# Linear attention and a PReLU feed-forward on one core: the order of the first loads, the layout of four solved values, and two engines changed in the opening stage

## The chip, the cores and the metric

The kernel runs on one core of a Trainium2 chip. The metric is the device time of one execution in microseconds; before the change the median of three runs is 665.36 us. The engines are named as in the profile: PE (TensorE; PEld is its weight load), DVE (VectorE), ACT (ScalarE), POOL (GpSimd) and SP (SyncE, which here only issues DMAs). A trailing q, as in SPq, is an engine's instruction queue.

## The reference

The first half is delta-rule linear attention over 4 batches, 8 heads, 768 tokens and head dimension 48; the second half is a feed-forward block with a learned negative slope on the 3072 tokens of width 384.

```python
k_n = k / (norm(k, axis=-1) + 1e-06)
for t in range(768):
    y[:, :, t] = einsum('bhd,bhde->bhe', q_t, state)
    v_old = einsum('bhde,bhd->bhe', state, k_t)
    state = state + beta_t * einsum('bhd,bhe->bhde', k_t, v_t - v_old)
x = y as (3072 tokens, 384)
h = x @ w_in                                   # 384 x 2048
g = maximum(h, 0) + alpha * minimum(h, 0)
out = g @ w_out                                # 2048 x 384
```

All is 32-bit floating point.

## The kernel before, in words

**Tiling.** The recurrence is cut into 12 chunks of 64 tokens (C = 64). A step n is one chunk of two batches, so there are 24 steps; steps 2c and 2c+1 are chunk c. Within a chunk the recurrence is a triangular system: it needs the products of the chunk's keys with each other, the inverse of a lower triangular matrix, and products with the state. When both steps of a chunk are through, `to_ffn` turns its 256 tokens, and the feed-forward of that chunk runs: `ffn_in` (PE L1070, then ACT L1080 and DVE L1082 for the slope) and `ffn_out`. Nearly all the time is this feed-forward on PE, into which the attention of later chunks is woven.

**Order.** All five engine queues are in the order in which the Python code calls the instructions (`manual_schedule`); an engine whose next instruction waits holds up all behind it. Semaphores are set by the framework from the tiles that an instruction reads and writes, buffers that share a tag among them.

**The opening stage** is the first 50 us or so. What matters of it, in program order:

- *First loads.* Keys (`load_early`), beta, queries (`load_q`), values (`load_v`) and 512 KB pieces of w_in (`fetch_in`) go out on SP, one queue. The slopes alpha (`al_sb`, L1668) go out after the sixth piece of w_in. `al_sb` shares the tag "prod" with the scratch tile that `eliminate_small` uses on DVE. `load_late` then fetches the keys a second time, in the layout that the state update needs (tile kl).
- *Keys.* For steps 0 to 3: square, transpose, products of the keys (L472), of which DVE and ACT pick the 16x16 blocks on the diagonal (`pick`) and ACT copies the rest (`raw`) into the tiles `beyond`, which live in `sums`; POOL multiplies them by beta (`weigh_below`, L640).
- *Slopes and queries.* `slopes` transposes alpha on PE (L335); then come the transposes of the queries (`flips`, L416), the products of queries and keys (`queries`, L1549), ACT's copy of them (L1555) and POOL's masking (L1559). `scale_first` (POOL, L840) multiplies the values of a step by beta.
- *`busy(BUSY)`* (L1534): BUSY products of 128x512 of tile kl with the identity, whose result nobody reads. A half in BUSY is a product of half the width. `short(n)` issues n such products of 32x32.
- *`begin_in(6)`*: the weights arrive as 64-bit words, whose two halves ACT converts (L227 the low one, L229 the high one); `convert` then has DVE shift (L243) and POOL add (L250) to finish a piece in two steps.
- *`eliminate_small`* inverts the 16x16 blocks on DVE: a transpose (L652), 14 pairs of a product (L669) and an addition (L675), ones on the diagonal (L681, on POOL), and a transpose back. `place_small(n, by_vector)` spreads the inverse of step n to its place by one DVE instruction (L698) or by four on ACT (L704).
- *`first_chunk`* solves steps 0 and 1: `matrix` (PE product, ACT copy L878), `own_values` (PE product, DVE copy L889), three rounds of `one_round` (PE product by L852, DVE addition L907), then `outputs` (L925). A product here is 16 matmuls, 32 rows in the profile. Half of the heads sit in the other half of the partitions, so a round needs its operands turned: `turn_matrix` makes the turned half of the matrix (two copies of 64x256), `turn_values` a second set of the values (one copy of 128x192 and two of 64x192), on ACT (L865) or POOL (L867) as the call says. `step_spaces` says where these tiles lie.
- *`second_pair`* does the same for steps 2 and 3, woven into the feed-forward of chunk 0. From step 4 on a different path (`attention`, `burst_a`, `burst_b`) is used; before each step there `scale_v` multiplies the step's 128x384 values by the norms (DVE, L778), 20 times in all.

The functions that the change touches, with the profile's line numbers:

## Time and profile before

| | before |
|---|---|
| median of three runs (lowest, highest) | 665.36 us (665.34, 666.39) |
| the profiled execution: time, span | 662.88 us, 661.1 us |
| PE busy in the span | 632.1 us (96%) |
| DVE, ACT, POOL busy | 483.4, 261.3, 136.7 us |
| first product of the keys' inverse (`matrix` of step 0) starts | 33.96 us |
| `matrix` of step 1 starts | 37.78 us |
| `outputs` of step 0 starts | 47.09 us |
| HBM traffic | 31.56 MB read, 4.72 MB written |

The span runs from the first to the last instruction of the program; the execution's own time is 1.78 us more. Times within the profile count from the start of the span. The profiled execution is 2.48 us below the median of the runs. A row of the timeline reads: start, duration, engine, line, operation, output<-inputs, partitions x elements, number merged into the row, and in brackets the idle time of the engine before it and what ended it.

### The profile page before, as it was taken

Reading aid. Unit: us, or ns where it says so; the run is one execution under the profiler, and the core shown is the slowest. Engines: PE = TensorE matmul, PEld = TensorE weight load, DVE = VectorE, ACT = ScalarE, POOL = GpSimd, SP = SyncE. Lnnn points to the kernel's source line nnn. Section 1 sums busy time; section 2 is a strip of 40 time slices with the busy share of each in tenths; the row PEclk is TensorE's granted clock in tenths of the full one; section 3 lists DMA queues with packets and bytes.
Section 4 is the critical chain, followed back from the end, with each engine's and each line's share of the span. In section 5 each row is a group of like instructions: output and inputs, shape, how many; then the busy total and the mean of one; then the engine's idle time right before and its main releaser. Section 6 shows DMA issues by size and latency. Waiting matters only on the chain.

```text
span 661.1 us, 21374 instructions
## 1 busy us (share of the span) xinstructions
PE 632.1 (96%) x9147; PEld 560.7 (85%) x9147; DVE 483.4 (73%) x1140; ACT 261.3 (40%) x610; POOL 136.7 (21%) x258
## 2 busy tenths in 40 slices
PE   5569998999999999999999999999999999999997
PEld 4367777656688988998998998988999999999997
DVE  5535779987899869758959748858968658568383
ACT  6366745434554252243343242232245245042140
POOL 5444744410000000001000000000035044053260
PEclk9979999999999999999999999999999999999999
DMA  9862854311332122122112112112111210100000
GB/s 212 206 177 51 225 126 120 83 28 32 66 77 51 26 54 45 26 50 49 28 38 37 27 37 38 26 38 38 26 42 33 43 34 2 29 10 1 25 1 25
DMA packets 111151, 37.67 MB, mean 57 GB/s; under 512 B 104224, under 2 KB 107440, under 8 KB 111056
## 3 DMA queue, kind: packets, MB, share of 16 engines
q1 hardware_dynamic: 109184, 35.81, 24.3%
q8 instruction: 72, 1.18, 0.7%
q10 hardware_dynamic: 1872, 0.49, 0.4%
q14 instruction: 23, 0.19, 0.1%
HBM read 31.56 MB, written 4.72 MB: 55 GB/s over the span
## 4 chain that ended last, share of the span: by engine, by line
PE 86%; DVE 5%; ACT 4%; SPq 2%; DMA 1%; issue 1%; POOL 0%; ACTq 0%; DVEq 0%; POOLq 0%
PE p_ffn L1070 22%; PE p_ffn L1135 17%; PE p_more L1387 8%; PE p_ffn L1113 5%; PE p_more L1303 5%; PE p_ffn L1293 3%; PE p_ffn L1387 3%; PE p_pair L416 3%; PE p_pair L801 2%; PE p_ffn L1298 2%; PE p_pair L741 2%; PE p_pair L925 2%; PE p_pair L912 2%; PE p_pair L852 2%; PE p_pair L472 2%; PE p_pair L789 1%
## 5 line engine op out<-in xcount | busy, mean ns | idle before, releaser
L1070 PE MATMUL p_ffn<-xt,w_in 128*128 128x256 f32 x768 | 176.5, 383 | 3.3 <-DVE sums L1082 1.6
L1070 PEld LDWEIGHTS p_ffn<-xt,w_in 128*128 128x128 f32 x768 | 142.2, 190 | 24.4 <-issue 2.3
L1082 DVE SCALAR_TENSOR_TENSOR act<-act,al_t,p_ffn 128x256 f32<-128x256 f32 x112 | 48.5, 474 | 26.2 <-ACT act L1080 26.0
L1080 ACT ACTIVATE act<-p_ffn 128x512 f32<-128x512 f32 x56 | 33.3, 595 | 83.2 <-PE p_ffn L1070 83.0
L1327 POOL TENSOR_TENSOR k_t<-k_t 128x128 f32<-128x128 f32 (+1 forms) x48 | 29.0, 604 | 166.4 <-ACT k_t L1322 163.9
L557 DVE TENSOR_TENSOR block<-block,prod 128x30 f32<-128x30 f32 (+9 forms) x150 | 54.2, 362 | 5.2
L551 DVE TENSOR_TENSOR prod<-block 128x30 f32<-128x30 f32 (+9 forms) x150 | 51.9, 346 | 1.6
L405 POOL TENSOR_TENSOR beta_t<-beta_t,rec 128x8 f32<-128x8 f32 x20 | 5.2, 260 | 225.0 <-DVE rec L399 215.4
L1135 PE MATMUL p_ffn<-w_out,act 128*128 128x192 f32 x288 | 49.6, 328 | 0.0
L1135 PEld LDWEIGHTS p_ffn<-w_out,act 128*128 128x128 f32 x288 | 46.6, 190 | 0.3
L968 ACT COPY xt<-p_pair 128x384 f32<-128x384 f32 x22 | 10.4, 479 | 90.8 <-PE p_pair L964 76.9
L1327 POOL TENSOR_TENSOR block<-block 128x128 f32<-128x128 f32 (+1 forms) x48 | 27.9, 582 | 17.3 <-ACT block L1322 14.8
L1293 PE MATMUL p_ffn<-xt,w_in 128*128 128x256 f32 x96 | 28.7, 380 | 0.0
L753 ACT COPY inv<-p_pair 32x256 f32<-32x256 f32 x40 | 14.5, 361 | 24.9 <-DVE u L916 24.1
L793 ACT COPY y<-p_pair 128x384 f32<-128x384 f32 x22 | 10.4, 479 | 33.0 <-PE p_pair L789 31.4
L1341 DVE SCALAR_TENSOR_TENSOR act<-block,al_t,act 128x256 f32<-128x256 f32 x32 | 19.1, 637 | 5.4 <-ACT block L1337 5.4
L1155 DVE TENSOR_TENSOR o_sb<-u,p_ffn 128x192 f32<-128x192 f32 x24 | 7.9, 350 | 20.5 <-PE p_ffn L1135 20.0
L820 DVE TENSOR_TENSOR r<-v_raw,p_pair 64x192 f32<-64x192 f32 (+1 forms) x60 | 21.2, 353 | 2.2 <-PE p_pair L801 1.2
L1341 DVE SCALAR_TENSOR_TENSOR act<-k_t,al_t,act 128x256 f32<-128x256 f32 x32 | 22.3, 735 | 0.1
L949 DVE TENSOR_TENSOR beside<-beside,p_pair 48x384 f32<-48x384 f32 (+1 forms) x36 | 19.8, 549 | 2.9 <-PE p_pair L941 2.7
L1387 PE MATMUL p_more<-w_out,act 128*128 128x192 f32 x128 | 21.9, 329 | 0.0
L1113 PE MATMUL p_ffn<-w_out,act 128*128 128x384 f32 x64 | 21.6, 490 | 0.0
(285 smaller groups left out, 1404.6 us busy)
## 6 DMA issues: line engine op xcount, KB each, us to landing
qp<-in_q_dram SPq DMA_DIRECT2D x48, 96.0 KB, 3.0
v_raw<-in_v_dram SPq DMA_DIRECT2D x48, 96.0 KB, 3.0
kl<-in_k_dram SPq DMA_DIRECT2D x96, 48.0 KB, 2.7
out_dram<-o_sb SPq DMA_DIRECT2D x90, 48.0 KB, 1.6
space_out<-in_moe_w_out_dram SPq DMA_DIRECT2D x11, 384.0 KB, 4.1
ke<-in_k_dram SPq DMA_DIRECT2D x43, 96.0 KB, 3.1
w_out<-in_moe_w_in_dram SPq DMA_DIRECT2D x6, 512.0 KB, 6.3
w_out<-in_moe_w_out_dram SPq DMA_DIRECT2D x5, 384.0 KB, 4.5
```

The costliest lines, as they stand in the source:

```text
L551: nc.vector.tensor_tensor(out=prod, in0=r[:, 0:j, j : j + 1].to_broadcast([128, j, n]), in1=r[:, j : j + 1, j + 1 : HB].to_broadcast([128, ...
L557: nc.vector.tensor_tensor(out=r[:, 0:j, j + 1 : HB], in0=r[:, 0:j, j + 1 : HB], in1=prod, op=ALU.add)
L1070: nc.tensor.matmul(p_h[:, i], w_in[:, t, (f + i) * 128 : (f + i + 1) * 128], xt[:, t], start=(t == 0), stop=(t == KT - 1),)
L1080: nc.scalar.activation(g, p_h, ACT.Relu, scale=-1.0)
L1082: nc.vector.scalar_tensor_tensor(out=g[:, i], in0=g[:, i], scalar=al_t[:, f + i : f + i + 1], in1=p_h[:, i], op0=ALU.mult, op1=ALU.add,)
L1113: nc.tensor.matmul(p_o[u], gs[f // 2][:, f % 2, u * 128 : (u + 1) * 128], w_out[:, f], start=(f == 0), stop=(f == FT - 1),)
L1135: nc.tensor.matmul(p, x(i), w(i), start=(i == 0), stop=(i == FP - 1))
L1293: nc.tensor.matmul(p[:, f * 256 : f * 256 + 256], w(2, f), xt[:, 2], start=True, stop=False)
L1303: nc.tensor.matmul(q[:, j], a, b, start=True, stop=True)
L1327: nc.gpsimd.tensor_tensor(out=dst, in0=a, in1=b, op=ALU.add)
L1341: nc.vector.scalar_tensor_tensor(out=g[:, f], in0=r[:, f], scalar=al_t[:, 2 * i + f : 2 * i + f + 1], in1=g[:, f], op0=ALU.mult, op1=ALU.add,)
L1387: nc.tensor.matmul(p, x(i), w(i), start=(i == 0), stop=(i == FP - 1))
```

## The change

- **Loads.** alpha goes out right after the first keys, into a piece of the tile `rest` of its own (shown as "turned" in the profile) and no longer into a buffer of the tag "prod". The values go out before all pieces of w_in; the pieces follow, six at once. Piece seven is asked for a little earlier.
- **Order on the engines.** ACT's negation of the mask `minus` and POOL's `weigh_below` for all steps stand earlier in the order; seven short products stand ahead of `busy`, and BUSY is 6.5 in place of 6.0. Five pieces of w_in are begun on ACT ahead of the solve, not six, and one at its end, not two; three are still finished in it, the steps of which stand at other places.
- **Elimination.** The ones on the diagonal are written by DVE after the last pair, not by POOL after the first.
- **Placing.** `place_small` of step 1 is by DVE; those of steps 2 and 3 stand in `first_chunk`, on ACT as before, not in `second_pair`.
- **Values in three parts.** The solved values z of steps 0 to 3 lie in one tile of three parts: even heads, odd heads, odd heads turned. A round reads parts 0 and 1 or, by a stride of two, parts 0 and 2, so that the copy of 128x192 in `turn_values` falls away and only two copies of 64x192 are left. They are no longer written back over the raw values, and turned matrices are made by other engines (step 0 on ACT, step 1 on POOL).
- **`scale_v`** runs on POOL.

```diff
 W_IN_P = 512
-BUSY = 6.0
+BUSY = 6.5
 EARLY = 8
...
     load_early(2, (nc.scalar, nc.sync))
-    al_sb = work.tile([FT, 128], FP32, name="al_sb", tag="prod", bufs=2)
...
             )
-            if j == 1:
-
-                ones = flat.rearrange("p (s e) -> p s e", s=2)[:, :, :: LB + 1]
-                nc.gpsimd.memset(ones, 1.0)
+        nc.vector.memset(flat.rearrange("p (s e) -> p s e", s=2)[:, :, :: LB + 1], 1.0)
         own = work.tile([128, NJ * H, HB], FP32, name="inverse", bufs=1)
...
             nv[n] = v_raw.pop(n)
-            nc.vector.tensor_tensor(
+            nc.gpsimd.tensor_tensor(
                 out=nv[n], in0=nv[n],
...
         m, turned_m, z, u = step_spaces[n]
-        z, u = (
-            x[:, 0 : H * D].rearrange("p (a g d) -> p a g d", a=2, g=G) for x in (z, u)
+        return (
+            m.rearrange("p (a g i) -> p a g i", a=2, g=G),
+            turned_m.rearrange("p (g i) -> p g i", g=G),
+            z.rearrange("p (a g d) -> p a g d", a=3, g=G),
+            u.rearrange("p (a g d) -> p a g d", a=2, g=G),
         )
-        m = m.rearrange("p (a g i) -> p a g i", a=2, g=G)
-        return m, turned_m[:, 0 : G * C].rearrange("p (g i) -> p g i", g=G), z, u
...
         crossing(p, [x[:, 0], x[:, 1]], rhs_[n], True)
-        return [lambda: nc.vector.tensor_copy(out=by_parity(nv[n]), in_=p)]
+        return [lambda: nc.vector.tensor_copy(out=step_space(n)[2][:, 0:2], in_=p)]
...
     def turn_values(n, engine):
-        z, turned_z = by_parity(nv[n]), step_space(n)[2]
-        copy_by(engine, turned_z[:, 0], z[:, 0])
-        swapped(engine, turned_z[:, 1], z[:, 1])
+        z = step_space(n)[2]
+        swapped(engine, z[:, 2], z[:, 1])
...
         p = region(p, G * D, g=G)
-        m, turned_m, turned_z, u = step_space(n)
-        z = by_parity(nv[n])
+        m, turned_m, z, u = step_space(n)
+        z, turned_z = z[:, 0:2], z[:, 0:3:2]
         if i == 2:
...
-    def unit(x):
-        return x.rearrange("p h c -> p (h c)")
-
-    step_spaces = {
-        n: [first_words[:, 2048 * n + at : 2048 * n + at + 512] for at in (0, 512, 1024, 1536)]
-        for n in range(2)
-    }
-    step_spaces[2] = [unit(x) for x in (inv[0], mid[0], inv[1], mid[1])]
-    step_spaces[3] = [unit(x) for x in beyond]
+    def step_words(x, at=(0, 512, 768, 1344)):
+        return [x[:, i : i + n] for i, n in zip(at, (512, 256, 576, 384))]
+
+    step_spaces = {n: step_words(first_words[:, 2048 * n :]) for n in range(2)}
+    step_spaces[2] = [
+        *step_words(first_words, (2560, 3648, 3072))[:3],
+        mid[0].rearrange("p h c -> p (h c)")[:, 0 : H * D],
+    ]
+    step_spaces[3] = step_words(sums.rearrange("p i s e -> p (i s e)"))
     for x in beyond:
...
         place_small(0, True)
-        place_small(1, False)
+        place_small(1, True)
...
-        def round_(n, i):
-            return one_round(n, i, ps_big()[:, :, 0:WY])
-
         now(matrix(0, ps_big()[:, :, 0 : G * C]))
-        convert(2)
+        convert(1)
+        turn_matrix(0, nc.scalar)
         z_0 = own(0)
-        m_1 = matrix(1, ps_big()[:, :, 0 : G * C])
         now(z_0)
         turn_values(0, nc.gpsimd)
-        now(m_1)
+        now(matrix(1, ps_big()[:, :, 0 : G * C]))
+        turn_matrix(1, nc.gpsimd)
         z_1 = own(1)
-        convert(1)
         now(z_1)
-        turn_matrix(0, nc.scalar)
         turn_values(1, nc.scalar)
-        convert(1)
-        turn_matrix(1, nc.scalar)
+        convert(2)
         for i in range(3):
-            rounds = [round_(n, i) for n in both]
+            rounds = [one_round(n, i, ps_big()[:, :, 0:WY]) for n in both]
             for x in rounds:
...
             if i == 0:
-                convert(2)
+                place_small(2, False)
+        convert(3)
         load_v(3)
-        begin_in()
+        place_small(3, False)
         y_0 = outputs(0, ps_big()[:, :, 0:WY])
...
     load_early(NKE)
+    al_sb = rest[:FT, 0:128]
+    nc.sync.dma_start(out=al_sb, in_=moe_alpha.rearrange("(f p) -> f p", p=128))
     for n in range(2):
         load_q(n)
-    fetch_in(4)
     for n in range(2):
...
     fetch_in(6)
-    nc.sync.dma_start(out=al_sb, in_=moe_alpha.rearrange("(f p) -> f p", p=128))
...
     norms(3)
+    first_roots(1)
     now(copy_3)
-    first_roots(1)
     gram_2 = gram(2)
...
     raw(1, gram_1)
+    fetch_in(7)
+    weigh_below(1)
     now(later_signs)
...
     load_v(2)
+    nc.scalar.mul(minus, minus, -1.0)
     for i in range(2):
...
     mask = queries()
-    weigh_below(1)
-    nc.scalar.mul(minus, minus, -1.0)
     for i in range(2):
...
         load_q(i + 2)
-
-    busy(BUSY)
-    begin_in(6)
-    eliminate_small()
     for n in range(2, NJ):
         weigh_below(n)
+
+    short(7, ps_one())
+    busy(BUSY)
+    begin_in(5)
+    eliminate_small()
...
             scale_first(i)
-            place_small(i, False)
         alongside(2, 1)
...
```

## The prediction

> **What bounds the kernel now.** I read the page first, for where PE is idle, then the chain of waits, the timeline of the opening stage, and counts of instructions by stretch.
>
> ```profile
> span 661.1 us, 21374 instructions
> ...
> PE 632.1 (96%) x9147; PEld 560.7 (85%) x9147; DVE 483.4 (73%) x1140; ACT 261.3 (40%) x610; POOL 136.7 (21%) x258
> ...
> q8 instruction: 72, 1.18, 0.7%
> ```
>
> PE is busy for 632.1 of 661.1 us. Of the 29 us left, PE's own list of waits has only 1.3 us after 104.5 us (0.6, 0.5 and 0.2), and from 44.61 to 104.5 us about 5 us. So the feed-forward runs at PE's pace, and what can be won lies before 45 us. My yardstick is the start of `outputs` of step 0 (PE L925), 47.09 us: what moves it moves the end, unless a later engine falls behind. The chain up to there:
>
> ```profile
> 14.78 3.70 SPq L210
> 18.48 0.04 issue
> 18.52 0.43 SPq L210
> 18.95 0.04 issue
> 19.00 4.47 DMA al_sb<-in_moe_alpha_dram
> ...
> 36.56 1.17 ACT inv L704 x4
> ...
> 42.76 1.85 issue
> ```
>
> Alpha, 8 KB, is issued at 19.00 us because SP has queued six weight pieces and the values ahead of it. PE, in order, stands on its transpose from 14.44 us, and the queries behind it wait too. Later the chain goes through ACT, which has twelve conversions of 0.6 to 0.7 us queued ahead of the four copies of L704. At 42.76 us PE stops for 1.85 us with nothing to wait for.
>
> ```profile
> 23.61 0.26 PE L335 MATMUL p_pair<-ident,al_sb 16*128 16x16 f32 x1 [9.16 <-DMA al_sb<-in_moe_alpha_dram]
> 23.90 0.27 DVE L669 TENSOR_TENSOR prod<-block 128x112 f32<-128x112 f32 x1 [2.54 <-PE p_pair L335]
> 27.98 5.39 PE L1534 MATMUL p_pair<-kl,ident 128*128 128x512 f32 x12 [0.33 <-DMA kl<-in_k_dram]
> 31.72 1.18 DVE L652 STREAM_TRANSPOSE inverse<-block 128x256 f32<-128x256 f32 x2 [3.34 <-POOL block L681]
> 37.78 1.13 PE L852 MATMUL p_pair<-inv,sums 64*64 64x64 f32 x32 [2.67 <-ACT inv L704]
> ```
>
> The reader should see four stalls that the change addresses: 9.16 us of PE; 2.54 us of DVE, because `al_sb` shares its scratch buffer; 3.34 us of DVE, because the ones on the diagonal queue on POOL behind the masking; and 2.67 us of PE. They are not in series, so their sum is not the gain.
>
> **The change, part by part.**
>
> *Alpha and queries.* Alpha is issued at 5.32 us; with its 4.47 us it lands before 10. The transpose then waits for its PSUM bank, which ACT's last copy of L645 frees at 16.32. So L335 moves from 23.61 to 16.4, and with it the query work (1.95 + 1.97 us) to an end at 20.4 and ACT's two copies L1555 to 21.6. ACT's ten conversions (0.67 + 0.68 us a piece, less overlap 6.4 us) end at 28, ahead of need. The negated `minus` (0.27 us) and `weigh_below` move within idle time of ACT (7.57 us before L336) and of POOL (6.13 us before L1559).
>
> *DVE's elimination.* It starts at 17.45 as before. Undisturbed, its 28 instructions take about 7.9 us by the rows (eight in 1.97, the last sixteen in 4.49, four between at about 0.32), so it would end at 25.3, not 28.39. But POOL's work moves under it: L840 (3.51 us) from 16.1, since the values land by 14; L1559 (2.50 us) from 21.1; two of L640 (1.7 us). The trace shows what this costs:
>
> ```profile
> 100.86 1.03 POOL L250 TENSOR_TENSOR w_out<-w_out 128x384 uint32<-128x384 uint32 x1 [1.26 <-ACT w_out L227]
> 100.92 1.08 DVE L557 TENSOR_TENSOR block<-block,prod 128x84 f32<-128x84 f32 x1
> ```
>
> A DVE instruction of 0.23 us takes 1.08, until POOL's ends. Under L840 at 19.45 to 21.36, DVE got four instructions done in 1.9 us, one for each of POOL's. With one per POOL instruction, 13 are done at 25.4 and the other 15 (4.2 us) at 29.6. Then ones on DVE (0.15 at most, POOL's price), the transposes 1.18, and L698 twice at 0.87: the inverse of step 0 at 31.8, of step 1 at 32.7, against 33.81 and 37.72 now. Without any blocking it would be 27.5; with POOL's 7.7 us all added, 35.2 for step 0. I take 31.8, worked out from the overlap that is shown.
>
> *The filler.* PE must finish `busy` before `matrix` of step 0. It reads tile kl, whose bytes follow the same transfers as before, so it lands only as much earlier as DMA wasted time: the DMA share from 18 to 20 us is low after the 3.70 us issue stall, and two pieces landed late. I put kl at 26.4, about midway between 25.5 (both losses made good) and 27.84 (as now). The filler's 13 half products cost 5.39/12 = 0.45 us each, 5.84 us, at full clock. But PE will have been idle from 20.9 to 26.4. After such idling the granted clock halves for 3.4 us:
>
> ```profile
> 38.00:41.00 3.00, 3.00 (x112) 2.89 (x112) 0.83 (x2) 2.12 (x6) 0.41 (x1) 0.50 0.92 313
> 42.00:44.50 2.50, 0.54 (x15) 0.40 (x13) 0.98 (x3) 1.06 (x2) 1.29 (x1) 1.00 0.76 293
> 45.00:48.00 3.00, 3.00 (x111) 3.00 (x107) 1.66 (x3) 0.00 (x0) 1.43 (x3) 0.50 0.25 51
> ```
>
> (Columns: stretch, length, then busy time and number for PE, PEld, DVE, ACT, POOL, then granted clock, DMA share, GB/s.) Both halved stretches follow a stop of PE of 2.67 or 1.85 us. One such stretch adds 1.7 us to the filler; I take one, with none to two for the range. `matrix` of step 0 thus starts at 26.4 + 5.84 + 1.7 = 34.0, as late as now (33.96): the filler takes over from DVE, which has 2 us to spare. By bounds: 32.0 (DVE) to 37.2 (27.98 + 5.84 + 3.4).
>
> *The chain.* `matrix` to `outputs` takes 13.13 us now. It holds ten products of 0.66 us at full clock (PE rows of 34.44 and 41.34), and DVE's additions (0.55) of one step lie beside the product of the other: 6.7 us. The wait of 2.67 us goes, since step 1's inverse no longer passes ACT. What fills DVE, ACT and POOL in between keeps its place: the conversions L243 (0.42), turned copies of 0.35 to 0.42 each, all within 0.1 us of need; the L704 of steps 2 and 3 (2.44 us) lie in ACT's idle 5.14 us ahead of its copy of y, and would cost their 2.44 us uncovered. The dropped copies of `turn_values` (0.47 on POOL, 0.35 on ACT, twice) are off the path: nothing.
>
> What does not go is the stop with no cause. 18294 PE instructions to 72 packets of queue q8 are 254 each, and up to the two such stops of PE that are over half a microsecond (1.85 at 42.76, 0.66 at 77.05) the counts are 943 and 2465, 1522 apart, six times 254. So PE runs out of instructions at block ends, where products are small and DMA is full. The seven short products and the half more (4 instructions each) add 32 ahead of the solve; the ends fall at the end of `matrix` of step 1, where the 2.67 us wait hid one before, and at the end of round 1 of step 0. I charge two stops at the mean of the two seen, 1.25 us each, and 0.7 us for a partly halved clock: 6.7 + 2.5 + 0.7 = 9.9 us. Bounds: 6.7, and 6.7 + 3 x 1.85 + 1.7 = 14.0.
>
> The Trainium skill ("Runtime: NRT & Kernel Launch", Instruction fetch mechanics) also has blocks of 256 instructions, but calls the cost of a boundary mostly hidden; the 1.85 us speak against that here. By that rule the sum would be 3.2 us less.
>
> *Afterwards.* ACT has one piece of w_in more to begin (1.35 us); its 2.65 us idle ahead of L793 at 60.67 hide that. The other engines follow PE as before: nothing, with 1 us either way.
>
> *`scale_v` on POOL.* 20 times 0.55 us leave DVE; POOL takes 20 times about 0.85 (L640, the same 128x384). PE waits 1.3 us in all after 104.5, so there is nothing to gain; a loss only if blocked DVE work reaches PE (third rival). Between -1.3 and +17 us, I take 0: DVE loses its own 0.55 and gets blocked for up to 0.85.
>
> **The sum.** 34.0 + 9.9 = 43.9 against 47.09: 3.2 us. The profiled time goes from 662.88 to 659.7, and the median, 2.48 above it, from 665.36 to 662.2.
>
> **Rivals.**
>
> - *No stops in the solve.* The chain takes 6.7 + 0.7, `outputs` starts at 41.4, and the time is 659.7; with the filler at full clock too, 658. For: 34 to 40 us may have less DMA traffic, as loads move forward. Against: all of the second half of w_in is still to come. Chance 0.20.
> - *The filler starts late and cold.* kl lands at 27.84 as now and two halved stretches follow: `matrix` at 37.2, `outputs` at 47.1, time 665.4. For: the bytes ahead of kl are the same. Against: SP no longer stops while DMA is short of work. Chance 0.15.
> - *`scale_v` blocks DVE: slower.* While POOL multiplies, a DVE elimination instruction waits up to 0.85 us, and the slopes (L1082) that PE needs stand behind it. If eight of the 20 reach PE in full, 6.8 us: 665.36 - 3.2 + 6.8 = 669.0; it decides from 4.5 us, five or six of them. For: the pair of rows at 100.86. Against: over the same stretches PE hardly waits for DVE. The Trainium skill ("SBUF — State Buffer", Who interferes with whom) has the rule: a DVE instruction with two SBUF inputs contends with a POOL instruction that reads SBUF, exclusively. The trace agrees, with 1.08 us for 0.23. Chance 0.13.
>
> That the change does not do what it says is small: its list of instructions has alpha ahead of the queries on SP and the ones on DVE.
>
> **Numbers.** My forecast has 0.52. A measurement of this kernel tells about 0.2%, 1.33 us. Faster: forecast and first rival, 0.72; same: second, 0.15; slower: third, 0.13. The range, 658.0 to 666.3, reaches from the first rival to a little over the second with one stop more; the forecast's own is 660 to 664.
>
> **What would show it.** Right: L335 near 16.4, no DVE wait on it, no DVE wait for POOL at the transpose; L669 and L675 stretched under L840 and L1559; L1534 from about 26.4 for over 7 us and the first L852 right at its end; no wait on L704; stops of PE marked issue within L852; L925 near 44 us; after 105 us PE's waits as now. Wrong: a `matrix` held by DVE, not by the filler; `outputs` before 41 or after 47 us; new PE waits for DVE after 150 us.

## The result

The changed kernel is slower: 667.90 us median (665.09 to 671.34, 20 runs) against 664.86 us for the kernel before on the same chips (662.56 to 666.66, 20 runs). The ratio is 1.0047, 95% interval [1.0032, 1.0062]: some 3.1 us more, where 3.2 us less were forecast. The profiled execution took 666.65 us (span 664.9), 3.77 us more than the one of before, so its profile can be used to look for the loss. It remains one execution of each kernel, of runs that spread over 4 to 6 us.

Busy time, share of the span and instructions of each engine on the page of the changed kernel:

```profile
PE 636.0 (96%) x9163; PEld 563.5 (85%) x9163; DVE 481.1 (72%) x1122; ACT 259.0 (39%) x603; POOL 152.1 (23%) x276
```

PE is busy for 3.9 us more than before (632.1), although it has only 16 more matrix rows. Of this, 3.2 us are the filler and the short products ahead of the solve (7.60 and 0.95 us for 5.39). What was lost, and where, has to be read from the places of the same product in both. PE's timeline in the opening stage (start, duration, engine, line, operation, and in brackets the idle time before):

```profile
16.50 0.28 PE L334 MATMUL p_pair<-ident,turned 16*128 16x16 f32 x1 [1.94 <-ACT sums L644]
...
29.34 7.60 PE L1530 MATMUL p_pair<-kl,ident 128*128 128x512 f32 x14 [7.88 <-DMA kl<-in_k_dram]
36.88 0.70 PE L848 MATMUL p_pair<-inv,sums 64*64 64x64 f32 x32
...
44.20 1.31 PE L848 MATMUL p_pair<-act 64*64 64x48 f32 x35 [2.72 <-issue]
...
47.08 1.57 PE L921 MATMUL p_pair<-u,a_t 64*64 64x48 f32 x32
```

Alpha's transpose is at 16.50 us as forecast, and the 9.16 us wait for alpha has gone. In its place PE waits 7.88 us for kl, the tile that the filler reads, and the solve starts at 36.88 us (33.96 before). The waits inside the solve are shorter, so that `outputs` starts at 47.08: the yardstick has not moved at all (47.09). What comes behind it has. The first L1066 of the feed-forward starts at 53.33 us (51.33 before); the one that waits for a slope of L1078 at 99.63 (96.15); the last wait of PE ends at 257.86 (253.98). So 2.0 us are lost between 47 and 53 us, 1.5 us up to 100 us, and 0.4 us later.

Stretches of the changed kernel behind the stop (length; busy time and number for PE, PEld, DVE, ACT, POOL; granted clock, DMA share, GB/s):

```profile
47.00:50.00 3.00, 2.98 (x64) 2.38 (x58) 0.92 (x3) 0.76 (x2) 1.71 (x2) 0.50 0.05 10
50.00:53.00 3.00, 3.00 (x62) 2.27 (x59) 0.56 (x1) 1.39 (x4) 2.58 (x6) 0.50 0.00 0
```

PE is busy throughout, at half the clock: from 43.17 to 53.41 us, 10.24 us on end, where the kernel before had 3.41 us behind its stop. That is the first 2.0 us. In the next stage PE runs out of instructions twice, and these two rows are 1.83 us against the 0.66 us of before:

```profile
79.44 0.69 PE L471 MATMUL p_pair<-k_t 48*64 48x64 f32 x30 [0.53 <-issue]
85.23 0.35 PE L471 MATMUL p_pair<-k_t 48*64 48x64 f32 x8 [1.30 <-issue]
```

### The profile page after: what moved, and what is told of

Read it like the earlier page. It is cut to its first block, busy times and chain, and to the rows that moved or that the text cites. A ratio compares the mean times of both kernels' runs of the same rounds, so it can differ in the third digit from the quotient of the medians.

```text
span 664.9 us, 21421 instructions
## 1 busy us (share of the span) xinstructions
PE 636.0 (96%) x9163; PEld 563.5 (85%) x9163; DVE 481.1 (72%) x1122; ACT 259.0 (39%) x603; POOL 152.1 (23%) x276
## 4 chain that ended last, share of the span: by engine, by line
PE 87%; DVE 4%; DMA 3%; ACT 2%; issue 1%; SPq 1%; POOL 0%; ACTq 0%; DVEq 0%; POOLq 0%
PE p_ffn L1066 22%; PE p_ffn L1131 17%; PE p_more L1383 8%; PE p_ffn L1109 6%; PE p_more L1299 4%; PE p_ffn L1289 3%; PE p_ffn L1383 3%; PE p_pair L415 2%; PE p_pair L797 2%; PE p_ffn L1294 2%; PE p_pair L737 2%; PE p_pair L921 2%; PE p_pair L908 2%; PE p_pair L471 2%; PE p_pair L848 1%
## 5 line engine op out<-in xcount | busy, mean ns | idle before, releaser
L1066 PE MATMUL p_ffn<-xt,w_in 128*128 128x256 f32 x768 | 176.3, 383 | 3.1 <-DVE sums L1078 1.6
L1066 PEld LDWEIGHTS p_ffn<-xt,w_in 128*128 128x128 f32 x768 | 142.7, 190 | 23.4 <-ACT space_out L228 2.0
L1078 DVE SCALAR_TENSOR_TENSOR act<-act,al_t,p_ffn 128x256 f32<-128x256 f32 x112 | 48.5, 474 | 27.8 <-ACT act L1076 27.6
L550 DVE TENSOR_TENSOR prod<-block 128x30 f32<-128x30 f32 (+9 forms) x150 | 55.1, 368 | 1.7
```

What stands on the lines that cost most here:

```text
L550: nc.vector.tensor_tensor(out=prod, in0=r[:, 0:j, j : j + 1].to_broadcast([128, j, n]), in1=r[:, j : j + 1, j + 1 : HB].to_broadcast([128, ...
L1066: nc.tensor.matmul(p_h[:, i], w_in[:, t, (f + i) * 128 : (f + i + 1) * 128], xt[:, t], start=(t == 0), stop=(t == KT - 1),)
L1078: nc.vector.scalar_tensor_tensor(out=g[:, i], in0=g[:, i], scalar=al_t[:, f + i : f + i + 1], in1=p_h[:, i], op0=ALU.mult, op1=ALU.add,)
```

## The experiments

Each kernel was timed in five rounds beside the kernel before on the same chip. The medians come from several chips, so kernels are best compared by the last column. "Shift" is the number of PE instructions ahead of the solve, against the changed kernel; it is +68 in e2, e5, e8, e9 to e12 and f6, 0 where nothing is said, and -32 in the kernel before.

| run | edit | median us (runs) | ratio to before, 95% |
|---|---|---|---|
| changed kernel | | 667.90 (20) | 1.0047 [1.0032, 1.0062] |
| e1 | scale_v on DVE | 666.73 (12) | 1.0026 [1.0005, 1.0047] |
| e2 | filler on an early key tile, 24 products | 681.57 (5) | 1.0244 [1.0221, 1.0267] |
| e3 | no filler, shift 0 | 663.41 (12) | 0.9965 [0.9945, 0.9985] |
| e4 | shift +128 | 664.71 (12) | 0.9989 [0.9971, 1.0008] |
| e5 | filler on turned keys, 24 products | 667.65 (10) | 1.0035 [1.0020, 1.0049] |
| e6 | e3 and late pieces | 661.70 (6) | 0.9940 [0.9916, 0.9964] |
| e7 | before, alpha early | 664.57 (12) | 0.9992 [0.9974, 1.0011] |
| e8 | e5, late pieces, scale_v on DVE | 667.34 (12) | 1.0029 [1.0013, 1.0046] |
| e9 | filler on turned keys, 8 products | 659.25 (6) | 0.9921 [0.9896, 0.9946] |
| e10 | e9, late pieces, scale_v on DVE | 659.28 (6) | 0.9915 [0.9890, 0.9940] |
| e11 | e10, POOL's work behind the elimination | 654.67 (4) | 0.9841 [0.9818, 0.9863] |
| e12 | e10 without filler | 657.43 (6) | 0.9890 [0.9867, 0.9913] |
| f1 | filler of before, shift -32 | 663.97 (12) | 0.9984 [0.9963, 1.0006] |
| f2 | load order of before | 667.93 (8) | 1.0042 [1.0025, 1.0059] |
| f3 | before, scale_v on POOL | 665.85 (12) | 1.0007 [0.9988, 1.0026] |
| f4 | f1 and scale_v on DVE | 664.70 (12) | 0.9993 [0.9975, 1.0011] |
| f5 | before, shift +32 | 666.39 (12) | 1.0019 [1.0006, 1.0033] |
| f6 | e11 without filler | 654.21 (4) | 0.9827 [0.9810, 0.9843] |

### scale_v: e1 and f3

```diff
-            nc.gpsimd.tensor_tensor(
+            nc.vector.tensor_tensor(
                 out=nv[n], in0=nv[n],
```

> The changed kernel with scale_v back on VectorE, nothing else. Theory A (the loss is made in the opening stage: filler held by kl, stop of PE, halved clock up to 53.41 us): all stages up to 105 us stay where they are (L921 at 47.1), only the 0.66 us wait of PE for a_t at 174.50 goes; 0.7 us less than the changed kernel, about 1.0035 times the kernel before. Theory B (scale_v on POOL blocks VectorE, which reaches PE): the whole 3.1 us go, ratio to the kernel before 1.000 or below.

f3 makes the opposite edit in the kernel before.

> The kernel before with scale_v on GpSimd and nothing else. Theory B in its small form: all is as before up to 105 us, one new wait of PE for a_t near 171 us of 0.6 us; 0.5 to 1.4 us slower, 1.001 to 1.002. Theory B in full: 3 us, 1.0047. Prediction's step: nothing, 1.000.

The mechanism is there. Two rows of the changed kernel, in order of time:

```profile
171.20 0.82 POOL L774 TENSOR_TENSOR v_raw<-v_raw,norm 128x384 f32<-128x384 f32 x1
171.21 1.08 DVE L550 TENSOR_TENSOR prod<-block 128x238 f32<-128x238 f32 x1
```

The DVE product, 0.40 us at the next size, takes 1.08 us beside `scale_v`, and PE then waits 0.66 us at 174.50 for a_t. That wait is in all changed kernels with scale_v on POOL, at 0.50 us in f3, and in none with it on DVE. One such wait reaches PE, not the eight of the rival. In the times nothing is certain: f3 is 1.0007 with an interval on both sides of 1, e1's interval overlaps that of the changed kernel, and f4 is not faster than f1. scale_v is not the cause of the 3.1 us: f1 and f4 below remove the loss with and without it.

### The filler: e2, e3, e5 and e8

```diff
-                x, ident, k_late[0].rearrange("p h d -> p (h d)")[:, 0 : x.shape[-1]]
+                x, ident, k_early[0].rearrange("p h d -> p (h d)")[:, 0 : x.shape[-1]]
```

(e2; BUSY 24.0.)

> The changed kernel with the filler reading the first early key tile, which has landed by 6.3 us, in place of kl, and 24 products in place of 6.5, so that PE works from 21.4 to about 31.8 us. Theory A: the first product L848 starts when VectorE has placed the inverse, at 32.0 us in place of 36.88; no halved clock ahead of it; the chain takes 6.7 us plus one stop of 1.25 to 2.72; L921 at 40 to 42 in place of 47.08; 5 to 7 us less than the changed kernel, 0.990 to 0.997 times the kernel before. Theory B: the opening gains the same, but nothing of the loss behind 105 us goes. Theory C (PE's idle time does not matter, only where the block of instructions ends): L848 at 32.0, the stop of 2.7 us somewhere else in the chain, and the clock halved behind it for 10 us all the same: L921 at 42, 3 us less than the changed kernel.

```profile
35.06 23.43 PE L1530 MATMUL p_pair<-ke,ident 128*128 128x512 f32 x48 [13.62 <-DMA ke<-in_k_dram]
```

A miss, by two errors that this row shows. The tile had landed by 6.3 us, but a later load fills it again, and that load stands ahead of the filler in program order: the filler waits for the new contents. And a product of 512 columns is two rows of 0.43 us, not one: 24 products are 48 rows. (The prediction's 13 "half products" are these rows, so its sum is not touched.)

e3 takes the filler away:

```diff
-    short(7, ps_one())
-    busy(BUSY)
+    short(14, ps_one())
```

> The changed kernel without the filler; seven more short products stand in for its instructions, so that the blocks of instructions end at the same products. PE then idles from 21.5 us to the first product of the solve. Theory A: L848 starts at 32.0 us in place of 36.88, the first 3.4 us of it at half pace (1.7 us lost), the stop of up to 2.7 us stays: L921 at 42 to 44, so 3 to 5 us less than the changed kernel and 0.997 to 1.000 times the kernel before. Theory D (the filler is what earns the full clock for the solve): the halved clock lasts through the solve, twice 6.7 us: L921 at 47 or later, no gain.

```profile
31.54 1.13 PE L848 MATMUL p_pair<-inv,sums 64*64 64x64 f32 x32 [9.20 <-DVE inv L694]
...
45.26 0.45 PE L921 MATMUL p_pair<-u,a_t 64*64 64x48 f32 x2 [3.75 <-issue]
```

The solve starts at 31.54 us, released by DVE's inverse and 5.3 us earlier than in the changed kernel; its first rows run at half pace (1.13 us for 32, not 0.70). The time drops by 4.5 us, with intervals that do not touch. So the filler that waits for kl is what holds the changed kernel back from being faster: the count of PE instructions is the same. Theory D is out.

e5 reads `k_t[0]` (the turned keys) instead, again with 24 products, and e8 adds two more edits.

> The changed kernel with the filler reading the turned keys of step 0 (112 rows, in place since about 10 us and reloaded by no transfer) in place of kl, 24 products. This is what the run with the first early key tile was meant to be: that tile is filled again by a transfer that stands ahead of the filler, so there PE waited 13.62 us for it. Theory A: PE works from 21 to about 31.8 us, L848 starts at 32.0 us with its 32 rows in 0.7 us (without filler 1.13), the chain then takes 8 to 10 us with stops of 1 to 3.75 us, L921 starts at 40 to 42; no halved clock, or a shorter one, behind it; 660 to 663 us, 0.990 to 0.996 times the kernel before. Theory C (idle time of PE does not matter): the first products are as slow as without filler, the halved clock of 7 to 10 us follows the stop all the same: as without filler, 663 us.

> The changed kernel with three edits that the theories point to: the filler of 24 products on the turned keys, the last four pieces of w_in asked for at the end of first_chunk, and scale_v on VectorE. Theory A with E: L848 at 32.0 us at full pace, stops of PE under 1.5 us in all of the solve, L921 at 39 to 40.5, no wait at 174.5 us; 656 to 660 us, 0.985 to 0.992 times the kernel before. If only A holds: as the filler on the turned keys alone, less 0.7 us: 660 to 662.

Both start the filler at 21 us without a wait, but have the same wrong length, so that the solve started at 44.10 and 44.02 us. Their times say nothing of the theories. Their solves do: e5's `outputs` follows 8.34 us after its start (10.2 in the changed kernel), with stops of 0.92 and 0.69 us, a full clock from 25.5 us on, and DMA moving 36 GB/s or less.

### DMA beside the stops: e6

```diff
-    fetch_in, begin_in, conv_in = weights(pieces, stages, ids, in_done, 0, True)
+    fetch_in, begin_in, conv_in = weights(pieces, stages, ids, in_done, 8, True)
...
         begin_in()
+        fetch_in(12)
```

> The changed kernel without the filler (seven short products for its instructions), and with the last four 512 KB pieces of w_in asked for at the end of first_chunk, not as the staging of earlier pieces comes free. Theory E (a stop of PE ends when a 16 KB packet of instructions on queue q8 lands, and that packet stands behind the pieces in the DMA engines): the stop of 3.75 us in L921, during which DMA moved 389 GB/s, shrinks to under 1.5 us, as in the run where DMA was idle in the solve (0.66 and 0.40 us); L921 of step 0 is through by 43 us in place of 45.7; 2 us or more less than the same kernel with early pieces, 0.993 times the kernel before. Rival (the packet comes late for another reason): the stop stays at 3 to 4 us. Against both, a price: the pieces now land 7 us or so later, at 55 to 60 us, and PE needs the last of them in the last quarter of the first L1066; if that comes too soon a wait of PE for DMA or ACT shows up behind 60 us.

```profile
42.19 0.45 PE L921 MATMUL p_pair<-u,a_t 64*64 64x48 f32 x2 [1.56 <-issue]
```

e6 is e3 with the last four pieces of w_in asked for later. The stops at the same two rows shrank from 1.10 and 3.75 us to 0.31 and 1.56. But the edit did not clear the DMA of pieces, since SP comes to the new place by 38.10 us: three pieces are issued from then to 39.72 us (four from 35.96 to 38.45 in e3), and in the stop of 1.56 us DMA moved 288 GB/s, against 339 in that of 3.75. So the shorter stops do not show theory E. For it speak e2, e5 and e8, whose stops fell into stretches with DMA at 8 GB/s or less and lasted 0.40 to 0.92 us; against it f3 below, with a stop of 2.05 us at 104 GB/s. PE did not wait for the late pieces. The medians, 661.70 and 663.41, have intervals that overlap; between e9 and e10 below, one of whose edits this is, there is no difference. What DMA traffic adds to a stop is open.

### The same filler in the right length, and none: e9, e10, e12

e9 has `short(23)` and 8 products on `k_t[0]`, so as many instructions as e5; e10 adds the late pieces of e6 and scale_v on DVE; e12 is e10 with `short(31)` and no filler.

> The changed kernel with the filler on the turned keys again, now in the right length: a product of 512 columns is two rows of 0.43 us, so 24 of them took 22.98 us and held the solve until 44.10. Here 23 short products and 8 long ones, as many instructions as with 24, about 2.6 + 6.9 us from 20.4 us, 1 to 3 us more if the clock is halved at the start. Theory A (the loss is the filler held by kl, and the idle PE): L848 starts at 31.5 to 32.5 us, its 32 rows in 0.7 us; the chain takes 8.3 us with stops of 0.9 and 0.7 as with 24 products, up to 4 us more since DMA moves pieces meanwhile; L921 at 40 to 44 (47.08 in the changed kernel); no stop of PE at 79 and 85 us, as with 24; 657 to 662 us, 0.988 to 0.996 times the kernel before. Theory C (only the places of the stops matter, not the idle time of PE): as with the kernel without filler, 663.

> The same filler of 8 products, with the last four pieces of w_in asked for at the end of first_chunk and scale_v on VectorE. Theory A with E (instruction packets stand behind pieces): L848 at 32, stops in the solve of 1 us at most each, L921 at 40 to 41.5; 0.7 us less behind 170 us; 655 to 659 us, 0.983 to 0.991 times the kernel before. If E does not hold with a warm PE: as the filler alone, less 0.7 us.

> The combined kernel with the 8 long products replaced by 8 short ones: as many instructions, but PE idles from 24 us to the solve at 31.9. Theory A (the filler pays because the clock is granted in full only to a PE that has worked): the first five products of the solve at half pace (1.13 for 0.69 us), 1.6 us, and a halved clock of 3 to 7 us behind a stop, 1.5 to 3 us: 2 to 4 us slower than the combined kernel with 8 long products. Theory C: within 1 us of it.

e9 came out as theory A said, 8.6 us faster than the changed kernel, though its shift of +68 may have a part in that. But e12 contradicts the reason that I gave. First rows of the solve and first rows behind its last stop, e10 and then e12:

```profile
31.81 0.69 PE L848 MATMUL p_pair<-inv,sums 64*64 64x64 f32 x32
...
41.31 0.26 PE L848 MATMUL p_pair<-r,act 64*64 64x48 f32 x2 [1.78 <-issue]
```

```profile
31.04 1.14 PE L848 MATMUL p_pair<-inv,sums 64*64 64x64 f32 x32 [7.49 <-DVE inv L694]
...
41.44 0.26 PE L848 MATMUL p_pair<-r,act 64*64 64x48 f32 x2 [1.77 <-issue]
```

With a warm PE the products take 0.69 us, without 1.14 us, and yet both come out of the last stop at 41.3 to 41.4 us. In both a 16 KB packet of instructions (queue q8) started to move at 38.9 us. In this pair the packets and not the pace of the products set when the solve is through. The packets do not come at fixed times, however: in e11 below the solve starts 2.9 us earlier than in e10, and its last stop ends 2.8 us earlier. The times are not told apart (0.9915 and 0.9890, intervals overlap): no gain from the filler is shown. Theory A's reason, a cold PE, falls; what remains of it is that the filler is in the way.

### Where instruction blocks end: e4, f1, f4, f5

e4 puts 39 short products ahead of the filler, in time in which PE waits for kl:

> The changed kernel with 39 short products in place of 7 ahead of the filler: 128 PE instructions more, all in time in which PE waits for kl (they take about 4.4 of the 7.88 us). The ends of the instruction blocks fall 128 instructions, half a block, earlier. Theory A: the filler still starts at 29.3 when kl lands, the idle time ahead of it is 3.5 us; if the stop of 2.72 us is the end of a block, it moves from the 29th row of round 1 to about 64 rows (two products of the solve) earlier, or falls away if the packet comes in time: L921 at 44.4 to 47.1, 0 to 4 us less than the changed kernel. Rival (the stop has another cause, bound to the place in the solve): it stays in round 1 with 2.7 us, and the time stays within 0.5 us.

The filler did not move (29.51), nor did the solve (36.88). The stop of 2.72 us went; stops of 1.90 and 3.37 us appeared, the first after the 30th row of round 0, 63 rows earlier, which with their weight loads are 126 instructions: the stop belongs to a block's end, not to a place in the solve. `outputs` started 2.3 us later (49.35), which neither expectation had, but the two stops at 79 and 85 us were gone. Net 3.2 us faster.

The packets of q8 settle what these stops wait for. In the twenty profiles kept, PE stops 52 times between 25 and 104 us for 0.3 us or more with nothing to wait for, and each of these stops ends 1.17 to 1.64 us after a 16 KB packet of q8 has landed.

f1 takes the change's own 32 instructions out:

```diff
-BUSY = 6.5
+BUSY = 6.0
...
-    short(7, ps_one())
     busy(BUSY)
```

> The changed kernel with the filler of the kernel before: 6 products, no short ones; 32 PE instructions less ahead of the solve, so that every block of instructions ends 32 instructions later. Theory F (where the blocks end costs the changed kernel 1 to 2 us behind the solve): the stops at 79 and 85 us change from 0.53 + 1.30 to under 0.7 in all; with the filler 0.4 us shorter 1.5 to 2.5 us less than the changed kernel, 1.001 to 1.0025 times the kernel before. Rival: only the 0.4 us of the filler, 1.004.

> The changed kernel with both scale_v on VectorE and the filler of the kernel before. If (a) and (b) together make the loss: 0.999 to 1.001 times the kernel before. If the loss lies elsewhere (kl, the halved clock behind the solve): 1.002 or more.

f1 is 3.9 us faster than the changed kernel, more than expected, with intervals that do not overlap, and level with the kernel before. Its stop and its stretches behind it:

```profile
43.97 0.77 PE L848 MATMUL p_pair<-act 64*64 64x48 f32 x18 [2.60 <-issue]
```

```profile
47.00:50.00 3.00, 2.50 (x61) 1.92 (x54) 1.12 (x3) 1.54 (x3) 2.27 (x3) 0.98 0.03 5
```

The stop is 16 rows later in the solve and as long, but the clock is whole again at 47.14 us: halved for 3.41 us, not 10.24. The first L1066 is at 50.94 (53.33), of which 0.36 us are the earlier start of the solve and 2.0 the clock. Behind it one stop of 1.01 us at 77.71 stands for the 1.83 us; at 254.52 us f1 leads by 3.34 us. f4 agrees (0.9993). So the loss goes with these 32 instructions and the shorter filler.

f5 is the test from the other side: the kernel before with eight tiny products in its wait for alpha.

```diff
     raw(3, gram_3)
+    short(8, big[-1][:, 0])
     slopes()
```

> The kernel before with eight products of 32x32 (32 PE instructions, as many as the change adds ahead of the solve) put ahead of the transpose of alpha, inside the 9.16 us in which PE waits for alpha. Nothing else differs. Theory F (the places where instruction blocks end decide): the stop in the solve moves from the 12th row of a product to about the 28th row of the one before, the clock behind it is halved for longer than 3.4 us, stops of more than the 0.66 us appear near 79 and 85 us; 2 to 4 us slower, 1.003 to 1.006 times the kernel before. Rival (the count does not matter; f1 gained by its shorter filler): 1.000, within 0.7 us.

```profile
44.54 1.31 PE L852 MATMUL p_pair<-act 64*64 64x48 f32 x36 [3.53 <-issue]
```

The stop moved to behind the 28th row as expected and was 3.53 us long, against 1.85; stops of 1.16 and 1.73 us stand at 79.05 and 85.27, where the kernel before had one of 0.66. The filler also ran longer, 7.76 us for 5.39, but `matrix` of step 1 started at 37.82 us all the same (37.78). The kernel is slower, by 0.19% [0.06, 0.33], though nothing was added but 32 instructions in idle time. That is less than the 2 to 4 us that I expected and than f1's step. So by this interval the count of instructions costs something, with its part of the 3.9 us of f1 between 0.4 and 2.2 us if the two kernels respond alike; how much of the rest is the 0.43 us of filler and how much the clock's phase is not settled.

How far can the lengths in one profile be trusted? f3 has the PE instructions of the kernel before, and its stops stand at the same rows:

```profile
46.09 0.77 PE L852 MATMUL p_pair<-act 64*64 64x48 f32 x19 [3.04 <-issue]
...
81.46 0.47 PE L472 MATMUL p_pair<-k_t 48*64 48x64 f32 x17 [2.05 <-issue]
```

They are 3.04 and 2.05 us long in place of 1.85 and 0.66. The places go with the count, the lengths differ from one execution to the next by more than a microsecond. The number of the stops is the firmer sign: with the changed kernel's count (also in e1, e3, e6, f2 and f5) there are two of over half a microsecond from 73 to 87 us, 1.8 to 2.9 us together; with that of the kernel before (also in f1, f3 and f4) one, of 0.66 to 2.05; with shift +128 or +68 none (e2, whose stages lie 20 us later, has one of 0.58 us at 99). Only e7 does not fit, with two.

More instructions need not cost. e12 is e6 with 17 more short products (shift +68) and scale_v on DVE, and it is the faster one, 0.9890 against 0.9940, with intervals that just do not touch. What scale_v does alone, between the kernel before and f3, cannot be told from zero.

### kl and the loads: e7 and f2

e7 is the kernel before with alpha asked for right after the first keys; f2 is the changed kernel with `fetch_in(4)` back ahead of the values.

> The kernel before with one part of the change alone: alpha is asked for right after the first keys, into a tile of its own. Theory A: the transpose of alpha and the queries move from 23.61 to 16.5 us as the prediction has it, but kl still lands at 27 to 28.5, so that PE idles 7 us ahead of the filler (0.33 before); the filler's first five products run at half pace, 1.7 us; the first product of the solve starts at 35 to 36 (33.96 before) and L921 at 48 to 49; 1 to 2 us slower, 1.001 to 1.004 times the kernel before. Rival (the prediction's step): kl lands at 26.4 since SP no longer stops; the solve starts at 34 or before; 0.997 to 1.000.

> The changed kernel with four pieces of w_in asked for ahead of the values again, as in the kernel before; alpha stays early. Theory L (values first make kl late): the fourth transfer of kl lands at 26.5 to 27.5 us in place of 27.6 to 29.4 (eight profiles with values first), the solve starts 1 to 2 us earlier, 1.002 to 1.003 times the kernel before. Rival (the bytes ahead of kl are the same and DMA moves them in the same time): 27.8 to 29.5, no change, 1.004 to 1.005.

```profile
29.62 7.57 PE L1533 MATMUL p_pair<-kl,ident 128*128 128x512 f32 x12 [9.03 <-DMA kl<-in_k_dram]
```

In e7 alpha's stall is gone and is a stall on kl, as theory A had it, with the solve at 37.12 us. The time is the same (0.9992), not 1 to 2 us more: the wait of 2.67 us in the solve closed as well. f2 changes nothing (1.0042; kl at 30.04): the values are not what makes kl late. Over seventeen profiles with alpha early the fourth transfer of kl landed at 27.6 to 30.0 us, never at the forecast 26.4; with alpha late (the kernel before, f3, f5) at 27.84 to 27.88. SP's own rows show a part of the reason. In e7 and f2 the queries' loads start 1.2 and 1.3 us later than before, behind alpha, and SP's stall on the fifth and sixth piece stays: their row takes 4.78 and 4.50 us (4.17 before), and from 18 to 20 us DMA moves 57 and 78 GB/s. In the changed kernel the stall has moved to kl itself (first the kernel before, then the changed one):

```profile
20.41 6.47 SPq L161 DMA_DIRECT2D kl<-in_k_dram  x8
```

```profile
17.53 11.62 SPq L161 DMA_DIRECT2D kl<-in_k_dram  x8
```

In the changed kernel each of these eight issues starts within 0.1 us of the landing of one of the eight pieces of w_in, the last of which lands at 28.54 us (26.27 before), and kl's transfers follow at once. What holds SP there is open.

### POOL under the elimination: e11 and f6

```diff
-    mask()
...
-    for n in range(2, NJ):
-        weigh_below(n)
...
         turn_matrix(1, nc.gpsimd)
+        mask()
+        for n in range(2, NJ):
+            weigh_below(n)
```

> As the combined kernel with 8 products, and in addition GpSimd's masking of the products of queries and keys (2.65 us) and its weighing of steps 2 and 3 (1.70 us) moved behind the turning of the matrix of step 1 in first_chunk, so that VectorE's elimination runs alone from 19.8 us; the filler is cut to 27 short and 4 long products to end by 28 us. Prediction's step (a VectorE instruction lasts as long as GpSimd's beside it): the five instructions that took 4.2 us from 21.67 to 25.83 take 1.4; the inverse is placed at 28.5 to 29.3 in place of 31.9 and L848 starts there; if nothing else binds, 2.5 to 3 us less than the combined kernel, 0.979 to 0.987 times the kernel before. Rivals: the packets of instructions come no earlier and take half of it back (1 to 1.5 us less); or the masking now holds up the outputs (L921 waits for POOL).

> The fastest kernel so far (GpSimd's work moved behind) with its 4 long products replaced by 4 short ones, so that PE idles from about 23.5 us to the solve. Theory G (the packets of instructions set the pace of the solve, so that half pace at its start costs nothing, as with and without filler in the combined kernel): the solve starts at 28 to 28.5, L921 within 0.5 us of 38.6; 653 to 656 us, 0.982 to 0.987 times the kernel before. Rival (the filler pays): 1.5 to 3 us slower than with it.

The same DVE instruction in the changed kernel, and in e11:

```profile
21.67 1.23 DVE L674 TENSOR_TENSOR block<-block,prod 128x108 f32<-128x108 f32 x1
```

```profile
21.17 0.27 DVE L674 TENSOR_TENSOR block<-block,prod 128x108 f32<-128x108 f32 x1
```

Four DVE instructions lasted until POOL's beside them had ended, 1.23, 1.23, 0.80 and 0.80 us; alone they take 0.27 to 0.28. The Trainium skill ("SBUF — State Buffer", Who interferes with whom) has this as an exclusive lock between a DVE instruction with two SBUF inputs and a POOL instruction that reads SBUF; the trace agrees. With POOL's work moved the solve starts at 28.89 us (31.81 in e10), 2.9 us earlier, and the median falls by 4.6 us, intervals apart; e11's filler is shorter, too. f6 against e12 is the same step without filler in either: the solve starts at 28.58 us (31.04), and the ratio falls from 0.9890 to 0.9827, intervals apart. f6 is as fast as e11, and at 654.21 us the fastest version here: 11.0 us below the kernel before, 13.7 below the changed one.

## Why the prediction was wrong, step by step

**Alpha and queries: right.** L334 at 16.50 (16.4), the queries through at 20.5 (20.4), ACT's conversions at 27.9 (28).

**The elimination: right.** Its last pair ended at 29.42 us (29.6), the inverse of step 1 at 31.96 (32.7). e11 shows that the stretching under POOL was worked out for the right reason.

**kl: the step that failed first.** It was put at 26.4 us, with "27.84 (as now)" as the late end, since its bytes follow the same transfers. It landed at 29.21, and in e1, with the same loads, at 27.62: so some 1.6 us of it differ between executions, but 26.4 was never reached. The bytes are the same; the time is not. The reasoning counted the DMA's idle time and not its rate, and took SP's stall as gone, where it had moved. One stretch of four microseconds (the last two columns are DMA share and GB/s), first of the changed kernel, then of the kernel before:

```profile
12.00:16.00 4.00, 2.56 (x69) 2.31 (x69) 3.65 (x13) 2.97 (x11) 3.09 (x8) 1.00 0.95 245
```

```profile
12.00:16.00 4.00, 2.44 (x69) 2.19 (x65) 3.65 (x13) 3.06 (x11) 3.09 (x8) 1.00 1.01 377
```

With the values ahead of all pieces 245 GB/s moved here for 377, and 128 for 218 in the four microseconds before: 0.9 MB less. From 16 to 20 us 0.8 MB were won back (328 and 371 GB/s for 184 and 96). Then the last two of the eight pieces came 2.57 and 2.13 us after the ones before them, the others 1.24 to 1.29. This is how kl came late in this profile, not why: f2, with 385 GB/s in the same stretch, has it later still. The late end of the forecast left out a loss without giving a reason; the cause of the delay stays open.

**The filler: right.** 7.54 us (29.34 to 36.88), against 5.84 + 1.7, the first products at half pace.

**The start of the solve** was therefore 2.9 us late (36.88 for 34.0), all of it kl. This is the second rival to a third of a microsecond (37.2 and 47.1; chance 0.15), by two errors of it that cancel: kl was 1.4 us later than its 27.84, and the filler lost one halved stretch, not two.

**The chain: right in its sum, not in its parts.** 10.2 us for 9.9, which is luck. One stop of 2.72 us, in round 1 of step 0 as named, did what two of 1.25 us were to do; the clock was 0.5 from 43.17. The ten products were put at 6.7 us by the length of their rows, but these overlap: the first four start at 36.88, 37.39, 37.84 and 38.37 us, so ten take about 5 at full clock. Two waits for DVE, 0.37 and 0.24 us, and a halved clock that cost more than the 0.7 us charged made up for it. The Trainium skill ("Runtime: NRT & Kernel Launch", Instruction fetch mechanics) has the crossing of a block mostly hidden; every run here has at least one stop of 0.66 us or more in its solve, up to 3.75 us, and each ends behind the landing of a packet; that speaks against it for products this small.

**Afterwards: the step that made the sign.** "Nothing, with 1 us either way" was 3.8 us between the two profiles. The yardstick failed with it: what moves `outputs` was to move the end, but it stood still (47.08 for 47.09) while the end moved by 3.8 us, and in e4 it came 2.3 us later than in the changed kernel though e4 is the faster one. I had counted block ends up to `outputs` and not behind, though the change moves every later one as well, and I had charged the halved clock 0.7 us inside the chain though it outlasted it. f1 shows both terms at about the size that the profiles give, 2.0 and 0.8 us, and f5 the sign; f3 shows that either can differ by as much from one execution to the next. Why the clock stays halved three steps of 3.41 us here and one in f1 is open. In all three profiles with the changed kernel's count and its filler (also e1 and f2) it was 10.24 us; with the count of before 3.41 (the kernel before, f1, f4) or 6.83 (f3, e7); 6.83 in f5. Whether the stop goes over the edge of a step does not decide it: in the changed kernel, f3 and f5 it does by over a microsecond, and 10.24, 6.83 and 6.83 us follow; in f1 and f2 by 0.25 and 0.22, and 3.41 and 10.24 follow. The Trainium skill ("TensorE: Matmul & The Clock Gate", Part 1: The HAM clock gate) has such a window of 3.4 us that runs free of the kernel; the steps in the trace agree.

**scale_v: right within the noise.** Taken at nothing, and f3 measures 1.0007 [0.9988, 1.0026]. Its rival named the mechanism and overstated how many such waits reach PE: one, of 0.66 us.

## What to carry to other kernels

Removing the largest wait gains only as much as the next wait on the same engine leaves: here the filler's operand, not the work, set the start of the solve, and a filler that waits for nothing, or none, was worth more than the whole change. Where an engine issues many small instructions, count them: 32 more in idle time moved the stops behind them and cost a measurable 0.2% in one kernel. Take the size of such a stop from more than one execution. And put POOL's work where DVE is not on the path: the 2.9 us of the elimination reached the end.

## What was not expected of the hardware

- All 52 stops of PE without a named wait, 0.3 us or longer, ended 1.17 to 1.64 us after a 16 KB packet of instructions had landed. At 0.69 or 1.14 us a product the solve left its last stop at 41.31 and 41.44 us.
- Behind a stop of PE of 2.72 us the clock was halved for 10.24 us, and behind one of 2.60 us for 3.41 us.
- With the same PE instructions, the stops at the same two rows were 1.85 and 0.66 us in one execution and 3.04 and 2.05 us in another.
